# Attention and gMLP mixer on one core: five warm-up multiplications, another order in the first block, one tile moved ahead of the first heads, and one store issued earlier

## The chip, the cores and the metric

The kernel runs on 1 core of one Trainium2 chip. The metric is the device time of one execution in microseconds (us); lower is better. The time given for a kernel is the median of several runs. Beside the timed runs there is one profiled execution, from which all views are taken.

## The reference

The input is one sequence `x` of 2048 rows and 1024 columns in bf16. Two branches read it, and a gate mixes them:

```
g = sigmoid((x * gate_w).sum(-1))
a = attention(x)  @ wo        # 32 heads of 32; each row sees 8 rows: itself, 2, 4, ... 14 back
z = gelu(x @ w_in)            # 2 * 1792 columns: z1 and z2
b = (z1 * (w_sp @ layernorm(z2) + b_sp)) @ w_out     # w_sp is 2048 x 2048
out = g * a + (1 - g) * b
```

## The kernel before, in words

Everything on the chip lies in one large SBUF tile, `arena`, of which named regions are used again and again. Most of the views therefore show operands as `arena`. TensorE (PE) does the products, ScalarE (ACT) mostly the evictions from PSUM with their nonlinear function, VectorE (DVE) the attention's products and sums and the sums that the fast matrix products need; nearly all DMAs are issued by SyncE (SP), in program order.

The order of all instructions is written out by hand (`manual_schedule`): an engine runs its instructions in the order in which the Python code emits them. A small planner, `Beat`, counts the columns that PE has been given and inserts the attention's DVE steps, loads and other small work when the count reaches their due time. It knows nothing of the run; it only fixes the order.

The opening, which most of the change touches, goes as follows.

- SP issues two row tiles of x (L924), then eight pieces of the weights `w2` of z2, one for each block of 128 input rows (L926), then six row tiles of x transposed on the way (L928), the weights of the first group of heads (`load_wg(0)`, L349, three loads), the other eight row tiles of x (L931), and further loads.
- `warm_up(n)` (L115) gives PE n multiplications of a zeroed tile, 128 by 512, whose results nobody reads. They start before any data are there.
- `turn(i, h)` (L353) transposes the row tiles 0 and 1 on PE into `xT`, four blocks at a time; ACT copies one half of each tile (L359), DVE the other (L361).
- `z2_block(blocks)` (L368) computes several tiles of z2 at once: for each of the eight blocks kt of input rows, one multiplication (L374) of 128 by 448 for each tile (i, c) of the list, each into its own PSUM bank; then one eviction with gelu for each (L383). i is the row tile, c a quarter of z2's columns. `z2_tile(i, c)` is the same with one tile: eight multiplications in a row.
- Then come the tiles (2,0) to (7,0) and (2,1), with `x_abs` on DVE (L387) between them, which sums the magnitudes of two row tiles at a time.
- `qkv_tile(0, j)` (L942) is the first group of heads, one row tile j after another: eight multiplications (L947), an eviction by ACT (L950) into a staging buffer, and after every fourth tile three stores to DRAM (L955).
- After j = 13, `x_scale` (L399) spreads the sum of all magnitudes over the partitions with a one-column multiplication (L401), and DVE works out a power of two from it (L394 to L403). `x_convert(u)` (L405, L406) then turns the row tiles 2u and 2u + 1 of `xT`, in place, into scaled f16. There are eight conversions, u = 0 to 7. From then on z2 tiles read the converted rows: tile (i, c) needs conversion i // 2 and no other.
- Behind the heads come three more tiles, (3,1), (6,1) and (7,1), the transpose of the gate weights (L989), and the heads of the groups 1 and 2, whose multiplications read rows of all eight blocks at a stride. Tiles (4,1) and (5,1) follow much later (L1034).
- `bank()` (L104) hands out PSUM banks from three pools in a rotation of four, one for each tile, so the number of tiles ahead of an instruction decides which pool it takes.

The attention's DVE steps begin at a due time that is set when the first heads are emitted; they read q, k and v from DRAM (L592 to L601).

The close is the product with `w_out`, in eight groups of two row tiles (L1342 to L1384). Each group makes four quarter results `o11`, `o12`, `o21`, `o22` (row tile by column half), whose last operation on DVE is L1369 for `o22` and `finish` (L1273) for the others; a row tile is stored when both of its halves are done (L1371, L1382). In the last group the second row tile is stored in parts: the half `o22` (L1373), and two quarters of `o21` (L1377, L1378), so that little is left behind the last multiplication.

Of the kernel before, what the change touches and what calls it, by code (L numbers as in the profile page):

```python
# [15 lines left out]
P = 128  # L16
S = 2048
D = 1024
# [22 lines left out]
NU = S // 256  # L41
# [16 lines left out]
def _sub_ap(t, offset_elems, dims):  # L58
    return bass.AP(tensor=t.tensor, offset=t.offset + offset_elems, ap=[list(t.ap[0])] + [list(d) for d in dims])
# [3 lines left out]
def kernel(  # L63
# [15 lines left out]
    out2 = out.rearrange("b s d -> (b s) d")  # L79
# [24 lines left out]
    def bank():  # L104
        taken[0] += 1
        pool, tag = ((seeded, "sd"), (psum, "ps"), (second, "pd"), (psum, "ps"))[taken[0] % 4]
        return pool.tile([P, 512], F32, name=tag, tag=tag)

    def two_banks():
        return (psum.tile([P, 512], F32, name="ps", tag="ps"), second.tile([P, 512], F32, name="pd", tag="pd"))  # L110
# [4 lines left out]
    def warm_up(n):  # L115
        pw = [seeded.tile([P, 512], F32, name="pw", tag="sd") for _ in range(2)]
        for r in range(n):
            nc.tensor.matmul(pw[r % 2][:], warm[:, 0:P], warm, start=True, stop=True)
# [185 lines left out]
    sync = nc.sync  # L304
# [48 lines left out]
    def turn(i, h):  # L353
        pt = psum.tile([P, 4, P], BF, name="pt", tag="ps")
        for k in range(4):
            nc.tensor.transpose(pt[:, k, :], xn[:, i, (4 * h + k) * P:(4 * h + k + 1) * P], ident[:])
        dst = xT[:, 4 * h:4 * h + 4, i * P:(i + 1) * P]
        if h == 0:
            nc.scalar.copy(dst, pt[:])  # L359
        else:  # L360
            nc.vector.tensor_copy(dst, pt[:])  # L361

    def z2_tile(i, c, wake=False):
        z2_block([(i, c)], wake=wake)
# [3 lines left out]
    def z2_block(blocks, wake=False):  # L368
        banks = [seeded.tile([P, 512], F32, name="sd", tag="sd") if wake else bank() for _ in blocks]
        for kt in range(KT):  # L370
            for ps, (i, c) in zip(banks, blocks):
                x = xh if converted[i // 2] else xT
                N = 512 if wake and kt == 0 else ZC
                nc.tensor.matmul(ps[:, 0:N], x[:, kt, i * P:(i + 1) * P],  # L374
                                 _sub_ap(w2, kt * W2P + ZC * c, [[1, N]]),
                                 start=(kt == 0), stop=(kt == KT - 1), skip_group_check=wake)
        for ps, (i, c) in zip(banks, blocks):
            scale = xinv if converted[i // 2] else 1.0
            z2_out(ps[:, 0:ZC], i, c, scale)
            beat.run(KT * ZC)  # L380

    def z2_out(src, i, c, scale):
        nc.scalar.activation(z2[:, i, ZC * c:ZC * (c + 1)], src, ACT.Gelu_apprx_tanh, scale=scale,  # L383
                             accum_out=s1[:, 4 * i + c:4 * i + c + 1])

    def x_abs(u):
        nc.vector.tensor_reduce(xl[:, u:u + 1], tokens[u].raw, AX.XY, ALU.add, apply_absolute_value=True)  # L387
# [355 lines left out]
    def vector_steps(t):  # L743
        for item in attention_steps(t):
            if not prep["done"] and prep["normed"] == 16 and beat.vector > prep["at"]:
                for h in range(2):
                    yield 0.0, 1.25, lambda h=h: scale_rows(0, h)
                for fn in s_sums(0):
                    yield 0.0, 0.7, fn
                for fn in t_sums():  # L750
                    yield 0.0, 2.0, fn
                prep["done"] = True
            yield item
# [132 lines left out]
    def load_rows_y(u):  # L886
        for r in range(2):
            sync.dma_start_transpose(rows[u % 5].whole[r], y_d[(2 * u + r) * P:(2 * u + r + 1) * P, :])
# [69 lines left out]
        projected[g] += 1  # L958
        beat.run(KT * 3 * C)

    warm_up(6)
    for i in range(2):
        for h in range(2):
            turn(i, h)
    z2_block([(i, c) for c in range(2) for i in range(2)])
    x_abs(0)
    for i in range(2, 8):
        z2_tile(i, 0)
        if i % 2 == 1:
            x_abs(i // 2)  # L970
    z2_tile(2, 1)
    beat.steps = vector_steps(beat.now + NJ * KT * 3 * C * BEAT + 8.0)
    for j in range(NJ):
        qkv_tile(0, j)
# [8 lines left out]
                converted[u] = True  # L983
    x_convert(7)
    converted[7] = True
    for i in (3, 6, 7):
        z2_tile(i, 1)
    pt = psum.tile([P, 4, P], BF, name="pt", tag="ps")
    nc.tensor.transpose(pt[:, 0, 0:KT], gw_r[:], ident[0:KT, 0:KT])  # L989
# [122 lines left out]
    def product(ps, w, v, c0, c1, first):  # L1112
        K = v.shape[1]
        for k in range(K):
            nc.tensor.matmul(ps[:, 0:c1 - c0], w[:, k, :], v[:, k, c0:c1], start=(first and k == 0),  # L1115
                             stop=(k == K - 1), skip_group_check=True)
        beat.run(K * (c1 - c0))
# [16 lines left out]
    def fork(ps, n, bias):  # L1134
        seed = seeded.tile([P, 512], F32, name="seed", tag="sd")
        if bias is None:
            nc.scalar.copy(seed[:, 0:n], ps[:, 0:n])
        else:
            nc.scalar.activation(seed[:, 0:n], ps[:, 0:n], ACT.Identity, bias=bias)  # L1139
        return seed  # L1140
# [66 lines left out]
    for n in range(2 * NU):  # L1207
        u, fb = n // 2, n % 2
# [52 lines left out]
    def y_sums(u):  # L1261
        v = rows[u % 5]
        TT(v.s1, v.a21, v.a22, ALU.add)
        TT(v.s3, v.a11, v.a21, ALU.subtract)
        TT(v.s2, v.s1, v.a11, ALU.subtract)
        TT(v.s4, v.a12, v.s2, ALU.subtract)
# [5 lines left out]
    def finish(out, ps, scale, x):  # L1272
        nc.vector.scalar_tensor_tensor(out, ps[:], scale, x, ALU.mult, ALU.add)  # L1273

    def halves(a, views):
        return [views[2 * a + h][:, 512 * c:512 * (c + 1)] for h in range(2) for c in range(2)]
# [59 lines left out]
    def hold(ps, scale):  # L1336
        out = keeps[kept[0] % 7]
        kept[0] += 1
        nc.scalar.activation(out, ps[:], ACT.Copy, scale=scale)
        return out  # L1340

    for u in range(NU):  # L1342
        v = rows[u % 5]
        lo, hi = [omr[:, 2 * u + h:2 * u + h + 1] for h in range(2)]
        m11, m12, m21, m22 = halves(u, mix)
        o11, o12, o21, o22 = halves(u, ob_slots)
        pa, pd = two_banks()
        if u == 0:
            for n in (2, 3, 4):
                load_rows_y(n)  # L1350
        product(pa, v.a11, d11, 0, 512, True)
        pb = fork(pa, 512, None)
        product(pd, v.s1, e1, 0, 512, True)
        p5 = hold(pd, hi)
        product(pa, v.s2, e2, 0, 512, False)
        u2 = hold(pa, lo)
        product(pb, v.a12, d21, 0, 512, False)
        finish(o11, pb, lo, m11)
        TT(u2, u2, m12, ALU.add)
        product(pa, v.s3, e3, 0, 512, False)  # L1360
        u3 = hold(pa, hi)
        if u == NU - 1:
            pe = seeded.tile([P, 512], F32, name="seed", tag="sd")
            nc.scalar.copy(pe[:, 0:256], pa[:, 256:512])
        TT(p5, p5, m22, ALU.add)
        if 0 < u < NU - 1:
            y_sums(u + 1)
        product(pd, v.s4, d22, 0, 512, False)
        TT(o22, p5, u3, ALU.add)  # L1369
        finish(o12, pd, lo, u2)  # L1370
        sync.dma_start(out2[2 * u * P:(2 * u + 1) * P, :], ob_slots[2 * u])  # L1371
        if u == NU - 1:
            sync.dma_start(out2[(2 * u + 1) * P:(2 * u + 2) * P, 512:D], o22)  # L1373
            for q, ps in enumerate((pa, pe)):
                sl = slice(256 * q, 256 * (q + 1))
                product(ps, v.a22, e4, 256 * q, 256 * (q + 1), False)
                nc.vector.scalar_tensor_tensor(o21[:, sl], ps[:, 0:256], hi, m21[:, sl], ALU.mult, ALU.add)  # L1377
                sync.dma_start(out2[(2 * u + 1) * P:(2 * u + 2) * P, sl], o21[:, sl])  # L1378
        else:
            product(pa, v.a22, e4, 0, 512, False)  # L1380
            finish(o21, pa, hi, m21)
            sync.dma_start(out2[(2 * u + 1) * P:(2 * u + 2) * P, :], ob_slots[2 * u + 1])  # L1382
        if u + 5 < NU:
            load_rows_y(u + 5)  # L1384
# [30 lines left out]
```

## Time and profile before

| | |
|---|---|
| median of 3 runs | 670.32 us (670.11 to 670.51) |
| profiled execution, its own time | 671.13 us |
| its span, first to last instruction | 669.3 us |
| PE busy | 662.7 us, 99% of the span |
| DVE busy | 575.1 us, 86% |
| ACT busy | 441.9 us, 66% |

A busy PE is not PE at its peak: multiplications are pipelined, and the view gives each with its full latency, so that rows of one engine overlap. The distance between the starts of two rows is what one takes from the engine. In a timeline row the columns are start, duration, engine, line, operation, tiles, shape and count; in brackets stands the idle time of the engine just before, and what ended it. PEld is the loading of weights, SPq the issue of DMAs. In the list of waits the numbers are us in total, times, and the longest. The program's end is 1.8 us longer than the span in the profiled execution (671.13 to 669.3).

### The profile page before, as it was taken

The numbers are of one execution on the slowest core, as the hardware profiler recorded it, in microseconds if no ns is written. First come the engines' busy times: TensorE is split into PE (matmuls) and PEld (weight loads), VectorE is DVE, ScalarE is ACT, GpSimd is POOL, SyncE is SP. The second block draws the span as 40 slices with busy tenths as digits, with TensorE's granted clock in tenths as the row PEclk, the third lists the DMA queues.
The fourth block names the chain that finished last, engine by engine and source line by source line (L and its number), as shares of the span: only waits on it lengthen the run. The fifth ranks groups of instructions, "written<-read, shape, count | busy, mean of one in ns | idle before, by whom it ended". The sixth has DMA issues, their size and how long they took to land.

```text
span 669.3 us, 9594 instructions
## 1 busy us (share of the span) xinstructions
PE 662.7 (99%) x3564; PEld 389.3 (58%) x3564; DVE 575.1 (86%) x660; ACT 441.9 (66%) x774; POOL 9.4 (1%) x68
## 2 busy tenths in 40 slices
PE   8999999999999999999999999999999999999998
PEld 4558877666777777555555555555555544444443
DVE  4567999999999999999999999999978788954745
ACT  4327577888879989889755568787767774522222
POOL 0000000000001000001000000000000000000000
PEclk9999999999999999999999999999999999999999
DMA  8999593354297996994966686648589599476211
GB/s 224 182 235 255 113 227 116 105 121 120 45 283 244 279 290 203 280 327 150 292 207 213 154 217 161 166 116 229 131 211 288 142 270 225 85 167 151 54 63 64
DMA packets 229919, 123.92 MB, mean 185 GB/s; under 512 B 191088, under 2 KB 217456, under 8 KB 229872
## 3 DMA queue, kind: packets, MB, share of 16 engines
q1 hardware_dynamic: 229872, 123.31, 69.7%
q8 instruction: 28, 0.46, 0.3%
q14 instruction: 19, 0.16, 0.1%
HBM read 63.97 MB, written 37.82 MB: 152 GB/s over the span
## 4 chain that ended last, share of the span: by engine, by line
PE 97%; ACT 1%; DMA 1%; SPq 0%; issue 0%; DVE 0%
PE ps L1115 25%; PE ps L947 17%; PE pd L1115 12%; PE ps L1098 7%; PE seed L1115 7%; PE sd L947 5%; PE pd L374 4%; PE ps L455 4%; PE sd L1098 4%; PE pd L1098 4%; PE pd L947 2%; PE pd L455 2%; PE ps L374 1%; PE sd L374 1%; PE seed L455 1%; DMA arena<-in_B_w_in_dram 1%
## 5 line engine op out<-in xcount | busy, mean ns | idle before, releaser
L1115 PEld LDWEIGHTS <-arena 128*128 128x128 f16 x1519 | 148.4, 98 | 154.4 <-issue 0.7
L1115 PE MATMUL ps<-arena 128*128 128x448 f16 (+1 forms) x864 | 186.1, 363 | 0.2 <-ACT seed L1139 0.2
L947 PEld LDWEIGHTS <-arena 128*128 128x128 f16 (+1 forms) x1024 | 141.6, 139 | 30.4 <-issue 1.2
L947 PE MATMUL ps<-arena 128*128 128x384 bf16 x704 | 128.7, 326 | 0.0
L1115 PE MATMUL pd<-arena 128*128 128x448 f16 (+1 forms) x432 | 95.6, 363 | 0.0
L1098 PEld LDWEIGHTS <-arena 128*128 128x128 f16 x512 | 50.0, 98 | 46.7
L514 DVE TENSOR_TENSOR arena<-arena 128x4096 bf16<-128x4096 bf16 (+1 forms) x64 | 74.0, 1157 | 1.7
L510 DVE TENSOR_TENSOR arena<-arena 128x8192 bf16<-128x8192 bf16 x16 | 70.8, 4422 | 5.0 <-DMA arena<-k_d 4.7
L577 DVE TENSOR_TENSOR arena<-arena,att_A 128x8192 bf16<-128x8192 bf16 x16 | 70.7, 4421 | 0.2
L950 ACT CAST arena<-ps 128x384 bf16<-128x384 f32 x88 | 43.0, 489 | 23.6 <-PE ps L947 21.4
L1098 PE MATMUL ps<-arena 128*128 128x448 bf16 x256 | 53.7, 353 | 0.0
L1115 PE MATMUL seed<-arena 128*128 128x448 f16 (+2 forms) x223 | 48.7, 361 | 0.0
L947 PE MATMUL sd<-arena 128*128 128x384 bf16 x224 | 41.0, 326 | 0.8 <-ACT arena L383 0.8
L374 PEld LDWEIGHTS <-arena 128*128 128x128 f16 (+1 forms) x256 | 24.9, 98 | 23.0 <-ACT arena L359 1.1
L583 DVE TENSOR_TENSOR arena<-arena 128x4096 bf16<-128x4096 bf16 x16 | 36.6, 2287 | 0.2
L374 PE MATMUL pd<-arena 128*128 128x448 bf16 x160 | 34.7, 353 | 0.0
L1273 DVE SCALAR_TENSOR_TENSOR arena<-seed,omr,arena 128x512 bf16<-128x512 f32 x8 | 6.0, 751 | 32.7 <-PE seed L1115 32.7
L455 PEld LDWEIGHTS <-arena 128*128 128x128 f16 x224 | 21.9, 98 | 18.1 <-issue 0.5
L767 ACT ACTIVATE arena<-arena 128x2048 bf16<-128x2048 bf16 x16 | 30.9, 1932 | 0.0
L894 ACT ACTIVATE arena<-arena 128x896 bf16<-128x896 bf16 x32 | 30.3, 947 | 0.5
L455 PE MATMUL ps<-arena 128*128 128x449 f16 x128 | 29.7, 354 | 0.0
L387 DVE TENSOR_REDUCE yl<-arena 128x1 f32<-128x2048 bf16 x8 | 18.3, 2286 | 13.1 <-DMA arena<-in_A_x_dram 13.0
(207 smaller groups left out, 845.9 us busy)
## 6 DMA issues: line engine op xcount, KB each, us to landing
arena<-in_B_w_sp_dram SPq DMA_DIRECT2D x16, 512.0 KB, 4.2
arena<-v_d SPq DMA_DIRECT2D x8, 960.0 KB, 6.0
z_d<-arena SPq DMA_DIRECT2D x16, 448.0 KB, 4.5
arena<-z_d SPq DMA_DIRECT2D x16, 448.0 KB, 3.6
y_d<-arena SPq DMA_DIRECT2D x16, 448.0 KB, 4.1
arena<-k_d SPq DMA_DIRECT2D x7, 960.0 KB, 6.7
arena<-in_A_wqkv_dram SPq DMA_DIRECT2D x24, 256.0 KB, 4.6
q_d<-arena SPq DMA_DIRECT2D x32, 128.0 KB, 2.1
```

Source lines behind the costliest of these rows:

```text
L374: nc.tensor.matmul(ps[:, 0:N], x[:, kt, i * P:(i + 1) * P], _sub_ap(w2, kt * W2P + ZC * c, [[1, N]]), start=(kt == 0), stop=(kt == KT - 1) ...
L455: nc.tensor.matmul(ps[:, 0:DN - 1], lhsT, v[:, k, 0:DN - 1], start=(first and k == 0), stop=(k == 3), skip_group_check=True)
L510: TT(prod.rearrange("p (w j c) -> p w j c", w=W, j=8, c=C), in0, in1, ALU.mult)
L514: return lambda: TT(pv[:, :, 0:n], pv[:, :, 0:n], pv[:, :, n:2 * n], ALU.add)
L577: TT(prod.rearrange("p (w j d h) -> p w j d h", w=W, j=8, d=DH, h=HG), in0, in1, ALU.mult)
L583: return [(4.4, mul), (2.3, lambda: TT(p3[:, 0:4, :], p3[:, 0:4, :], p3[:, 4:8, :], ALU.add)), (1.2, lambda: TT(p3[:, 0:2, :], p3[:, 0:2, ...
L767: nc.scalar.activation(slot, slot, ACT.Abs, accum_out=l1[:, a:a + 1])
L894: nc.scalar.activation(waste, g_ring[n % 4][:, r], ACT.Abs, accum_out=yl[:, k:k + 1])
L947: nc.tensor.matmul(ps[:, 0:3 * C].rearrange("p (t c) -> p t c", t=3), lhsT, wgt[:, :, kt, :], start=(kt == 0), stop=(kt == KT - 1))
L950: nc.scalar.copy(st[:, j % 4, :].rearrange("p (t d h) -> p t d h", t=3, h=HG), ps[:, 0:3 * C].rearrange("p (t h d) -> p t d h", t=3, h=HG))
L1098: nc.tensor.matmul(ps[:, 0:512 if whole and kt == 0 else ZC], xh[:, kt, i * P:(i + 1) * P], _sub_ap(w1, kt * ZC, [[1, 512 if whole and kt ...
L1115: nc.tensor.matmul(ps[:, 0:c1 - c0], w[:, k, :], v[:, k, c0:c1], start=(first and k == 0), stop=(k == K - 1), skip_group_check=True)
```

## The change

Four edits. The warm-up has five multiplications instead of six. In the first block of z2 the four tiles are listed row tile by row tile, (0,0), (0,1), (1,0), (1,1), instead of column by column. The tile (3,1) is computed ahead of the first heads, behind (2,1), instead of behind them; it then reads the rows unconverted, and the PSUM banks of the sixteen heads are shifted by one. In the last group of the close, the half row tile `o22` is stored as soon as it is computed, ahead of the operation that finishes `o12` and of the store of the first row tile.

```diff
-    warm_up(6)
+    warm_up(5)
     for i in range(2):
         for h in range(2):
             turn(i, h)
-    z2_block([(i, c) for c in range(2) for i in range(2)])
+    z2_block([(i, c) for i in range(2) for c in range(2)])
     x_abs(0)
     for i in range(2, 8):
         z2_tile(i, 0)
         if i % 2 == 1:
             x_abs(i // 2)
-    z2_tile(2, 1)
+    for i in range(2, 4):
+        z2_tile(i, 1)
     beat.steps = vector_steps(beat.now + NJ * KT * 3 * C * BEAT + 8.0)
     for j in range(NJ):
         qkv_tile(0, j)
...
     x_convert(7)
     converted[7] = True
-    for i in (3, 6, 7):
+    for i in range(6, 8):
         z2_tile(i, 1)
...
         product(pd, v.s4, d22, 0, 512, False)
         TT(o22, p5, u3, ALU.add)
+        if u == NU - 1:
+            sync.dma_start(out2[(2 * u + 1) * P:(2 * u + 2) * P, 512:D], o22)
         finish(o12, pd, lo, u2)
         sync.dma_start(out2[2 * u * P:(2 * u + 1) * P, :], ob_slots[2 * u])
         if u == NU - 1:
-            sync.dma_start(out2[(2 * u + 1) * P:(2 * u + 2) * P, 512:D], o22)
             for q, ps in enumerate((pa, pe)):
```

Because the planner's count of PE columns stands one tile higher when the attention's due time is set, the order on DVE differs in one place: five small operations for the scale of w_in's second half (L394 to L397, L433) come ahead of one of the attention's folds (L514) instead of behind it. On ACT the eviction of (3,1) moves with its tile. Everything else keeps its order.

## The prediction

> **What bounds the kernel now.** I read the page first: busy shares, then the chain that ended last.
>
> ```profile
> PE 662.7 (99%) x3564; PEld 389.3 (58%) x3564; DVE 575.1 (86%) x660; ACT 441.9 (66%) x774; POOL 9.4 (1%) x68
> PE 97%; ACT 1%; DMA 1%; SPq 0%; issue 0%; DVE 0%
> ```
>
> PE is on the path for 97% of the span. What PE skips, or waits, is therefore the currency; other engines matter where they make PE wait. The waits of PE say where that is:
>
> ```profile
> PE pw L118 <- DVE arena L113: 1.2, 1, 1.2
> PE ps L374 <- DMA arena<-in_B_w_in_dram: 1.1, 2, 0.9
> PE sd L947 <- ACT arena L383: 0.8, 1, 0.8
> PE ps L1115 <- ACT seed L1139: 0.2, 1, 0.2
> ```
>
> There are four places only, three of them in the first 24 us. The change touches the stretch of each of these three and the last stores. So a gain has a ceiling of a few us; a loss needs a new wait.
>
> **Warm-up and order of the first block.** The timeline of the opening, the source view of the transposes, and the chain:
>
> ```profile
> 1.18 2.74 PE L118 MATMUL pw<-arena 128*128 128x512 bf16 x6 [1.18 <-DVE arena L113]
> 2.87 0.15 PEld L118 LDWEIGHTS <-arena 128*128 128x128 bf16 x1 [0.28 <-issue]
> 3.38 0.11 PEld L356 LDWEIGHTS <-arena 128*128 128x128 bf16 x1 [0.36 <-DMA arena<-in_A_x_dram]
> 3.72 1.16 PE L356 MATMUL pt<-ident,arena 128*128 128x128 bf16 x16
> L356 PE MATMUL pt<-ident,arena x16: 219/220/314, 3.7 to 4.7; 128*128 128x128 bf16 x16
> 4.24 1.07 ACT L359 COPY arena<-pt 128x512 bf16<-128x512 bf16 x2 [2.24 <-PE pt L356]
> 5.82 0.35 PE L374 MATMUL ps<-arena 128*128 128x448 bf16 x1 [0.94 <-DMA arena<-in_B_w_in_dram]
> 6.00 0.35 PE L374 MATMUL pd<-arena 128*128 128x448 bf16 x1
> 7.14 0.35 PE L374 MATMUL sd<-arena 128*128 128x448 bf16 x1
> 7.70 0.35 PE L374 MATMUL ps<-arena 128*128 128x448 bf16 x1 [0.20 <-DMA arena<-in_B_w_in_dram]
> 2.60 5.05 DMA arena<-in_B_w_in_dram
> ```
>
> A warm-up multiplication occupies PE for 0.43 us (weight loads from 1.58 to 2.87 are 0.43 apart; the last shows here). Without the sixth, PE is free at about 3.29. The transposes' weights could be loaded from 3.38, when x landed, so the transposes begin about 3.45 instead of 3.72 and their copies end about 0.25 earlier than 4.24 + 1.07 = 5.31. Nobody waits for those copies: the first multiplication starts at 5.82 on the first piece of w2, and the third piece, issued at 2.60, lands at 7.65 and restarts PE at 7.70. Neither piece waits for PE. **Removed warm-up: 0.** Its cover is the 0.94 us wait.
>
> Row tile by row tile means: in each of the eight rounds the order becomes (0,0), (0,1), (1,0), (1,1). The 32 multiplications and four results are the same; only the first two now need tile 0 alone. Tile 1 was ready by 5.31 too, half a microsecond ahead of the data. **Reordering: 0.** The bounds of both together are −0.3 (if the earlier transposes did reach PE) and +1.1 (the clock, a rival below).
>
> The clock: the trace has the first transpose at 314 ns and a median of 220, so the full clock came while the transposes started, about 3.9 us. By the 0.43 us for 512 columns, 448 columns cost 0.376 before that; from 5.82 on the spacing is 0.19. Eight multiplications fit ahead of 7.70 as long as no more than two are at the slow clock, so the grant may come as late as about 6.57. That is 2.6 us of cover.
>
> **One z2 tile moved from behind the first heads to ahead of them.** Timeline around both places, and the DMA of the heads' weights:
>
> ```profile
> 21.31 1.68 PE L374 MATMUL ps<-arena 128*128 128x448 bf16 x8
> 23.02 0.54 ACT L383 ACTIVATE arena<-ps 128x448 bf16<-128x448 f32 x1 [0.88 <-PE ps L374]
> 23.78 1.46 PE L947 MATMUL sd<-arena 128*128 128x384 bf16 x8 [0.80 <-ACT arena L383]
> 17.39 1.48 SPq L349 DMA_DIRECT2D arena<-in_A_wqkv_dram  x1
> DMA to landing us min/median/max: 6.3/6.3/6.3
> 41.98 0.17 PE L401 MATMUL ps<-rs_n,rs_b 128*128 128x1 bf16 x1
> 43.10 5.38 DVE L406 TENSOR_SCALAR arena<-arena,x_sc 128x2048 f16<-128x2048 bf16 x8
> 44.42 1.41 DVE L406 TENSOR_SCALAR arena<-arena,x_sc 128x2048 f16<-128x2048 bf16 x2
> 44.56 0.52 PEld L374 LDWEIGHTS <-arena 128*128 128x128 f16 x4 [0.18 <-DVE arena L406]
> 44.60 1.68 PE L374 MATMUL sd<-arena 128*128 128x448 bf16 x8
> 46.12 1.68 PE L374 MATMUL ps<-arena 128*128 128x448 bf16 x8
> 47.63 1.68 PE L374 MATMUL pd<-arena 128*128 128x448 bf16 x8
> 49.35 1.52 PE L947 MATMUL ps<-arena 128*128 128x384 bf16 x8
> ```
>
> Tiles follow each other by 1.51 us (46.12 to 47.63). Tile (2,1) begins at 21.31, so PE could take the next at 22.82; it waits until 23.78, a hole of 0.96. The view blames ACT, but the first head writes a bank that was read long before; what it does read are the three weight loads of L349, the last issued at 17.39 and landing 6.3 later, 23.69. So the hole is a DMA wait and a tile whose data are there fills it. Moved there, (3,1) runs 22.82 to 24.33, past the landing. **The heads start 0.55 later** (24.33 for 23.78), and all that hangs on them.
>
> Behind the heads the three tiles stood for a reason that the rows show. The scaling of x starts from the one-column multiplication L401 behind the fourteenth head; eight conversions on DVE follow from 43.10, each about 0.66 behind the last, 0.75 long. (3,1) reads block 1, converted at 44.42 + 1.41 − 2 × 0.66 = 44.51, and PEld starts at 44.56: just in time. (6,1) and (7,1) read block 3. It is the fourth conversion: it starts with the second of the x2 row, 44.42 + 0.66 = 45.08, and ends at 45.83, just before PE asked at 46.12. In the changed kernel everything from L401 is 0.55 later, so block 3 is ready at 46.38 and the weight load can start at about 46.43, the multiplication at 46.47. The heads end at 44.60 + 0.55 = 45.15. **A new wait of 1.32 us** of PE for DVE, at the first z2 tile behind the heads. What is queued behind it is all of PE's program: (7,1), the transposes of the gate weights, and every head of the second group.
>
> Sum at the second group's first head (now 49.35): +0.55 for the later start, +1.32 for the wait, −1.51 for the tile no longer there = **+0.36 us**. The conversion of the last block (43.10 + 5.38 + 0.55 = 49.03) is done before the 49.71 at which it is then asked for, so no second wait follows. The ends for the new wait are 0 (nothing is waited for) and 3.98 (a wait for all eight conversions, 49.03 + 0.10 − 45.15). I take 1.32: the 0.05 from 44.51 to 44.56 shows that the wait is on the one conversion needed.
>
> What else moves with the tile: its eviction on ACT, to a stretch where ACT waits 0.88 for every tile; the rotation of PSUM banks by one for sixteen heads; and, by the hand-kept order, five small DVE operations (the scale of w_in's second half) one fold earlier. SP's order is unchanged up to the last stores.
>
> ```profile
> 47.84 0.48 ACT L950 CAST arena<-sd 128x384 bf16<-128x384 f32 x1 [7.78 <-PE ps L374]
> 57.63 4.42 DVE L510 TENSOR_TENSOR arena<-arena 128x8192 bf16<-128x8192 bf16 x1 [4.74 <-DMA arena<-k_d]
> 75.75 1.80 ACT L437 ACTIVATE arena<-arena,yl 128x1800 f16<-128x1800 bf16 x1 [4.80 <-DVE yl L395]
> ```
>
> The thirteenth head's eviction stands until 47.84 on a staging buffer, and the transposes at about 49.5 now take its bank; it is free at 48.32, 1.2 us of cover. The attention on DVE starts at 57.63 on a DMA, 4.74 after DVE had run dry, so 0.55 on DVE costs it nothing. The fold's swap lets the conversions at 75.75 start up to 1.2 earlier, which PE doesn't wait for. These are 0. And as PE waits nowhere between there and L1115's 0.2 us, the 0.36 arrives at the end whole.
>
> **The last half row tile stored first.** The tail in narrow windows:
>
> ```profile
> 663.75 0.69 DVE L1369 TENSOR_TENSOR arena<-arena 128x512 bf16<-128x512 f32 x1 [0.28 <-ACT arena L1339]
> 664.54 0.75 DVE L1273 SCALAR_TENSOR_TENSOR arena<-pd,omr,arena 128x512 bf16<-128x512 f32 x1
> 665.36 0.33 SPq L1371 DMA_DIRECT2D out_dram<-arena  x1
> 665.78 0.38 SPq L1373 DMA_DIRECT2D out_dram<-arena  x1
> 666.07 0.48 DVE L1377 SCALAR_TENSOR_TENSOR arena<-seed,omr,arena 128x256 bf16<-128x256 f32 x1 [0.21 <-PE seed L1115]
> 666.25 0.40 SPq L1378 DMA_DIRECT2D out_dram<-arena  x1
> 666.75 0.41 SPq L1378 DMA_DIRECT2D out_dram<-arena  x1
> ```
>
> SP issues one after the other with 0.09 between (665.36 + 0.33 to 665.78; 666.25 + 0.40 to 666.75 is 0.10). The last store's data are ready at 666.55, and SP takes 0.07 from DVE's end to an issue (664.54 + 0.75 to 665.36), so it could go at 666.62: SP's queue holds it 0.13 us. In the changed kernel the half tile, ready at 664.44, is issued at about 664.51, in a stretch where SP waits; the row tile keeps 665.36, the first quarter goes at about 665.93, the last one at 666.62. **Gain 0.12.** Bounds: 0 (the bytes in flight, not the issue, set the landing) and 0.4 (one issue fewer ahead).
>
> **Sum.** 0 + 0 + 0.36 − 0.12 = +0.24 us. The profiled execution has a span of 669.3 and took 671.13 with what lies around; the median of the runs is 670.32, 0.8 below it. On the median: 670.56, a change of 0.04%. About 0.2%, 1.34 us, is what a measurement of this kernel can tell from no change.
>
> **Rivals.**
> *No new wait* (chance 0.10). If the conversions were early enough for (6,1), the filled hole stays as a gain: −0.96 − 0.12 = −1.08, 669.24. For it: the hole is real. Against it: L401 stands behind the fourteenth head in PE's order, and a tile's 1.51 between heads and (6,1) is gone.
> *Slower: the clock* (0.15). One mechanism: with PE idle about 0.1 us ahead of the transposes and 1.2 after them, the grant is not there when the first block starts. In the trace it came about 2.76 us after the first warm-up multiplication (1.18 to 3.94). Counted anew from 5.82 it comes at 8.58, after seven at 0.376 each; the eighth ends about 8.77 where PE went on at 7.70: +1.07, with the rest +1.31, 671.63. It decides from a grant later than 6.57. Against it: PE starts at the same 1.18 and works nearly without a gap to 4.6.
> The Trainium skill (TensorE: Matmul & The Clock Gate, "What's actually happening") speaks against this edit in the same place: the clock is released by activity in free-running windows of about 3.4 us, not by a count of multiplications, so less work there can miss a window. By that, as an estimate, a missed window would move the grant from 3.9 to 7.3 and cost four slow multiplications, +0.4; the trace shows one grant and no window.
> *The edits don't reach the end* (0.07): tail bound by bytes, new wait half as long, 0.2 us of slack at L1139 taken up; −0.3 to 0, 670.0 to 670.3.
> *Forecast* (0.68): 670.56, own range 670.1 to 671.0.
>
> **The numbers.** The range 669.5 to 671.7 leaves out the first rival and the far tails. Over 0.2% faster needs the first rival and 0.26 more, such as the 0.3 of a freed opening: half its chance, 0.05. Over 0.2% slower needs the clock's +1.31 with a trifle more, or a wait for all conversions: 0.12. The rest, 0.83, is within.
>
> **What would show it.** In the changed profile: PE's waits lose the 0.8 us at L947 and gain about 1.3 us at L374 behind the heads, for DVE L406; the first head at about 24.33; L401 at 42.53; (6,1) at 46.47; the second group at 49.7; first multiplication of z2 still at 5.82 and again at 7.70; the last store 0.1 us earlier relative to the last DVE operation. A first block with 0.376 spacing behind 5.82, a wait at L374 under 0.5 us, or a w2 piece landing with another time would prove the forecast wrong.

## The result, and the profile after

The changed kernel takes 671.13 us (median of 22 runs, 670.01 to 673.18), the kernel before 670.15 us (22 runs, 669.61 to 671.02). The ratio is 1.0015, 95% interval 1.0008 to 1.0022: slower by 0.15%, about 1.0 us. The forecast was +0.24 us, 670.56, with 670.1 to 671.0 as its own range and 669.5 to 671.7 as the outer one. The time lies in the outer range and above the forecast's own, the sign is the forecast one, and the size is four times the forecast. (A ratio is worked out over the runs of both kernels and is not the quotient of the two medians, so the two can differ by some hundredths of a per cent.)

The profiled execution of the changed kernel took 672.64 us with a span of 670.9, against 671.13 and 669.3 before. Its waits of PE:

```profile
PE pw L118 <- DVE arena L113: 1.2, 1, 1.2
PE ps L374 <- DVE arena L406: 1.1, 1, 1.1
PE ps L374 <- DVE arena L361: 0.6, 1, 0.6
PE ps L1116 <- ACT seed L1140: 0.2, 1, 0.2
```

The wait ahead of the first head is gone, the new one for the conversions (L406) is there, and the wait at the start of the first block is now for a copy (L361), not for w2. The timeline of PE in the opening:

```profile
1.18 2.31 PE L118 MATMUL pw<-arena 128*128 128x512 bf16 x5 [1.18 <-DVE arena L113]
3.52 1.89 PE L356 MATMUL pt<-ident,arena 128*128 128x128 bf16 x16
5.98 0.53 PE L374 MATMUL ps<-arena 128*128 128x448 bf16 x1 [0.57 <-DVE arena L361]
6.30 0.58 PE L374 MATMUL pd<-arena 128*128 128x448 bf16 x1
6.67 0.58 PE L374 MATMUL ps<-arena 128*128 128x448 bf16 x1
...
9.29 0.40 PE L374 MATMUL pd<-arena 128*128 128x448 bf16 x1
9.52 0.35 PE L374 MATMUL ps<-arena 128*128 128x448 bf16 x1
9.71 0.35 PE L374 MATMUL sd<-arena 128*128 128x448 bf16 x1
```

This is the clock, a rival of the prediction: the transposes take 1.89 us instead of 1.16, and the first block's multiplications are 0.37 apart until 9.29, then 0.19. The full clock came at about 9.4 us in this execution, where the first profile had it at 3.9. PE is 1.45 us late from here on (tile (2,1) starts at 22.76 instead of 21.31). Now the place of the moved tile and of the conversions:

```profile
22.76 1.68 PE L374 MATMUL ps<-arena 128*128 128x448 bf16 x8
24.28 1.68 PE L374 MATMUL sd<-arena 128*128 128x448 bf16 x8
25.79 0.49 PE L947 MATMUL ps<-arena 128*128 128x384 bf16 x2
...
45.31 1.46 PE L947 MATMUL sd<-arena 128*128 128x384 bf16 x8
47.90 1.69 PE L374 MATMUL ps<-arena 128*128 128x448 bf16 x8 [1.12 <-DVE arena L406]
49.42 1.68 PE L374 MATMUL pd<-arena 128*128 128x448 bf16 x8
```

The last early head starts at 45.31 and is done 1.30 later, at 46.61; (6,1) starts at 47.90. The wait is 1.29 us; 1.32 was forecast. (The view counts 1.12, from the latency end of the row before.) At the tail, the issues of SP and the last operation of DVE:

```profile
666.25 0.33 SPq L1372 DMA_DIRECT2D out_dram<-arena  x1
667.10 0.33 SPq L1374 DMA_DIRECT2D out_dram<-arena  x1
667.85 0.48 DVE L1379 SCALAR_TENSOR_TENSOR arena<-seed,omr,arena 128x256 bf16<-128x256 f32 x1 [0.21 <-PE seed L1116]
668.36 0.33 SPq L1380 DMA_DIRECT2D out_dram<-arena  x1
```

From the start of the last DVE operation to the last issue it is 0.51 us (667.85 to 668.36), where it was 0.68 (666.07 to 666.75), and to the end of the span 3.02 instead of 3.27 (the spans are 670.86 and 669.34 with two decimals). So this one execution adds up: +1.45 in the opening, +0.34 at the second group's first head (51.14 there, 49.35 before, less the 1.45), −0.25 at the tail. That is +1.54 for a span that grew by 1.52. But 672.64 is the third longest of the 22 runs, and the sum of one execution is not the sum of the median. That is what the experiments had to separate.

### The profile page after: what moved, and what is told of

Its sections match the earlier page's. It is cut to its first block, busy times and chain, and to the rows that moved or that the text cites. A ratio compares the mean times of both kernels' runs of the same rounds, so it can differ in the third digit from the quotient of the medians.

```text
span 670.9 us, 9591 instructions
## 1 busy us (share of the span) xinstructions
PE 664.7 (99%) x3563; PEld 390.1 (58%) x3563; DVE 574.9 (86%) x660; ACT 443.1 (66%) x774; POOL 9.4 (1%) x68
## 4 chain that ended last, share of the span: by engine, by line
PE 98%; ACT 1%; DVE 1%; issue 0%
PE ps L1116 25%; PE ps L947 17%; PE pd L1116 12%; PE ps L1099 7%; PE seed L1116 7%; PE sd L947 5%; PE pd L374 5%; PE ps L455 4%; PE sd L1099 4%; PE pd L1099 4%; PE pd L947 2%; PE pd L455 2%; PE ps L374 2%; PE sd L374 1%; PE seed L455 1%; DVE arena L406 0%
## 5 line engine op out<-in xcount | busy, mean ns | idle before, releaser
L514 DVE TENSOR_TENSOR arena<-arena 128x4096 bf16<-128x4096 bf16 (+1 forms) x64 | 74.0, 1157 | 1.7
L1128 ACT ACTIVATE arena<-ps,bt 128x448 f32<-128x448 f32 x32 | 20.2, 632 | 13.9 <-PE ps L1116 13.4
```

The source lines that it names most:

```text
L514: return lambda: TT(pv[:, :, 0:n], pv[:, :, 0:n], pv[:, :, n:2 * n], ALU.add)
```

## The experiments

First each edit by itself. **Only the warm-up**, on the kernel before:

```diff
-    warm_up(6)
+    warm_up(5)
```

> The kernel before with five warm-up multiplications and nothing else changed. Theory A (the clock): with one multiplication less the full clock comes a whole window later in part of the executions, the transposes and the first block then run at 0.107 and 0.376 us a piece for some us. It expects about +0.7 us on the median (0.3 to 1.2), a spread of the runs over 2 us where the kernel before had 1.4, and a fastest run no slower than the fastest before. Theory B (the moved tile carries all of it): 0, within 0.2.

Measured: 669.85 us to 670.05 before, ratio 1.0000, interval 0.9991 to 1.0009; 669.47 to 670.76 in eleven runs. The clock as the cause of the median, theory A, is out. Its own profile shows why the missing multiplication need not cost anything:

```profile
5.64 0.53 PE L374 MATMUL ps<-arena 128*128 128x448 bf16 x1 [0.28 <-ACT arena L359]
5.97 0.58 PE L374 MATMUL pd<-arena 128*128 128x448 bf16 x1
6.34 0.58 PE L374 MATMUL ps<-arena 128*128 128x448 bf16 x1
6.71 0.53 PE L374 MATMUL sd<-arena 128*128 128x448 bf16 x1
7.08 0.35 PE L374 MATMUL ps<-arena 128*128 128x448 bf16 x1
...
21.45 1.68 PE L374 MATMUL ps<-arena 128*128 128x448 bf16 x8
22.97 1.46 PE L947 MATMUL sd<-arena 128*128 128x384 bf16 x8
```

The clock came at about 7 us and cost next to nothing, since the block still ended about where it did. And the last two rows show something that the forecast had not reckoned with: tile (2,1) starts at 21.45, the first head at 22.97, 1.52 later. There is no hole ahead of the heads here.

**All but the warm-up**: the changed kernel with `warm_up(6)`.

> The changed kernel with the six warm-up multiplications put back. Theory A: what is left is the wait behind the heads and the tail, +0.35 - 0.2 = +0.1 to +0.3 us, with the spread of the kernel before. Theory B: nearly all of the change's +1.0 us stays.

Measured: 671.14 us, ratio to before 1.0014 (1.0005 to 1.0023). The whole loss is there with all six warm-up multiplications; its profile has the clock by 6.7 us and the same 1.1 us wait for L406.

**Only the tile**, on the kernel before:

```diff
-    z2_tile(2, 1)
+    for i in range(2, 4):
+        z2_tile(i, 1)
...
-    for i in (3, 6, 7):
+    for i in range(6, 8):
```

> The kernel before with tile (3,1) moved ahead of the first heads and nothing else changed. Theory A: +0.36 us: a wait of 1.3 us for the fourth conversion behind the heads, against 0.96 us of hole filled. Theory B: +1.0 or more. A third possibility, that the wait in the profile is paid for by time that PE loses elsewhere anyway, expects -0.9 to 0.

Measured: 671.05 us, +1.0, ratio 1.0017 (1.0008 to 1.0025). The moved tile carries the loss: the "+1.0 or more" of theory B, not the +0.36 of the forecast. Tenths of a us are beyond these medians of eleven runs: this kernel, without the earlier store, should lie above "all but the warm-up" by what the store is worth, and lies 0.09 below it.

**Only the order of the block and the store**:

> The kernel before with the other order in the first block and the half row tile stored first, nothing else changed. Theory A and B alike: the order 0, the store -0.1 to -0.2 us. If the order by row tiles matters for the opening, the first multiplication of the first block starts earlier than 5.8 us or the block ends earlier than 12.2 us.

Measured: 669.88 us, −0.17, ratio 1.0000 (0.9991 to 1.0009). By the medians alone the difference is not clear of the noise; the tail shows it in all fourteen profiles: from the start of the last DVE operation to the end of the span it is 3.27 or 3.28 us in the five profiles with the old order of stores, and 3.01 to 3.03 in the nine with the new one. The store is worth 0.25 us. In this run's profile the first block starts at 6.09 and waits for w2, which is issued as before.

Then theory C was formed: the hole of 0.96 us that the tile was to fill is not there in most executions, and so the wait of 1.3 us is paid in full. **The kernel before once more**, for its profile:

> The kernel before once more, for its profile alone. Theory C: the heads' weights are there when PE gets to them, no hole ahead of the first head (the first profile had 0.96 us). Theory D: the hole is there again.

The issue of the last of the three weight loads, what the view of that tensor says of landing, and PE's rows:

```profile
16.83 1.60 SPq L349 DMA_DIRECT2D arena<-in_A_wqkv_dram  x1
```

```profile
DMA to landing us min/median/max: 5.3/5.3/5.3
```

```profile
21.02 1.68 PE L374 MATMUL ps<-arena 128*128 128x448 bf16 x8
22.53 1.46 PE L947 MATMUL sd<-arena 128*128 128x384 bf16 x8
```

No hole: the last weights are issued at 16.83 and land 5.3 later, at 22.13, ahead of the 22.53 at which PE asks. In the first profile it was 23.69 against 22.82. Worked out in the same way for all fourteen profiles, the weights land ahead of the end of tile (2,1) in twelve, in those of the kernels with the moved tile too; they are late in the first profile and in one further below (e12). This execution took 669.87 us, 1.26 less than the first profiled one, and the hole of 0.96 is most of that.

**The wait taken away**, on the changed kernel, by working the scale out two heads earlier, which the sum of x permits:

```diff
-        if j == 13:
+        if j == 11:
             x_scale()
-            for u in range(7):
+            for u in range(6):
                 x_convert(u)
                 converted[u] = True
+        if j == 13:
+            x_convert(6)
+            converted[6] = True
```

> The changed kernel with the scale of x worked out behind the twelfth head instead of the fourteenth: conversions 0 to 5 start about 2.6 us earlier, conversion 6 follows the fourteenth head and 7 the sixteenth as before. Theory C (the moved tile costs because its 1.51 us of cover behind the heads turn into a wait for the fourth conversion, while the hole that it was to fill is an accident of single executions): no wait at L374 behind the heads, the second group starts about 1.3 us earlier than in the changed kernel relative to the first heads, and the time falls by 1.1 to 1.3 us below the changed kernel, to about the kernel before or 0.2 below it. Theory D (the wait only shows where time is lost anyway; the cost is the shift of all later work against DVE and the DMAs): the wait goes, the time stays at +1.0.

Measured: 669.66 us to 670.12 before, ratio 0.9998 (0.9989 to 1.0006). The loss of 1.0 us is gone, and 0.46 of the medians' difference lies on the other side, though the interval spans no change. Its PE waits hold no L406 any more, and the tile follows the heads at once:

```profile
42.55 5.38 DVE L406 TENSOR_SCALAR arena<-arena,x_sc 128x2048 f16<-128x2048 bf16 x8
```

```profile
45.35 1.46 PE L947 MATMUL sd<-arena 128*128 128x384 bf16 x8
46.65 1.68 PE L374 MATMUL ps<-arena 128*128 128x448 bf16 x8
48.16 1.68 PE L374 MATMUL pd<-arena 128*128 128x448 bf16 x8
```

From the first head to the second group's first head it is 24.05 us here and 25.35 in the changed kernel: the 1.3 of the wait. So the cost was the wait itself; theory D falls.

**Only the order of the conversions**, block 3 first, on the changed kernel:

```diff
-            for u in range(7):
+            for u in (3, 0, 1, 2, 4, 5, 6):
```

> The changed kernel with the conversion of block 3 first, ahead of 0, 1, 2, 4, 5, 6. Theory C: (6,1) starts at once, but the second group needs all eight conversions, which end 5.4 us after the first starts; a wait of 0.8 to 0.9 us appears at its first head, and only about 0.5 us is won of the changed kernel's loss: +0.5 us to before. If the order alone were the fault, all of it, 1.3 us, would come back.

Measured: 670.41 us to 670.12, ratio 1.0007 (0.9998 to 1.0016). By the medians some 0.7 of the loss comes back and 0.3 stays, though the interval reaches no change; in the profile 0.6 comes back (24.76 us from the first head to the second group's, for 25.35). The wait turns up where it was expected, smaller than reckoned:

```profile
PE ps L947 <- DVE arena L406: 0.6, 1, 0.6
```

The second group needs all eight conversions: 1.1 us from L401 to the first (41.98 to 43.10 in the first profile) and 5.4 from there, 6.5 in all. Two heads of 1.30 us and two tiles of 1.51 give 5.6 of cover, three tiles 7.1. That is what the third tile was worth behind the heads.

**One warm-up multiplication**, on the kernel before, to size the clock:

> The kernel before with one warm-up multiplication instead of six. It measures the clock term: if the grant of the full clock follows PE's work by windows, one multiplication leaves PE idle until 3.4 us, the grant comes more often behind 7 us, and the median rises by 0.5 to 1.5 us with a spread over 2 us. If the grant doesn't depend on the warm-up, 0.

Measured: 671.15 us, +1.0, ratio 1.0018 (1.0010 to 1.0026), 669.83 to 673.02. In its profile the spacing of the first block falls from 0.37 to 0.19 only at about 8.5 us. So the warm-up does its work. Over all runs with five multiplications (four kernels) 6 of 55 lay 1.4 us or more above the median of their set; with six (six sets of variants and five of the kernel before) it was 3 of 194. Of the six, the two that have a profile, the changed kernel's first and e7's, show the clock at 9.4 us. For the other four, and for the three with six multiplications, the cause is inferred, not shown.

Last, a version without the wait and with the full warm-up, in three forms on one chip. **Early scale, tile ahead, six warm-ups**:

> The changed kernel with the early scale of x and six warm-up multiplications again. Theory C with the clock as a matter of single executions: the median as with five, 0.25 to 0.5 us below the kernel before (the tail is worth 0.25), and no run over 1 us above its own median, where 6 of 55 runs with five warm-ups lay 1.4 us or more above. If five warm-ups cost every execution something, the median falls further, by 0.3 us or more.

Measured: 669.92 us to 670.72 before, ratio 0.9987 (0.9978 to 0.9996), 669.14 to 670.42. It is faster than the kernel before on the same chip, and no run is 1 us over its median; the changed kernel, at a ratio of 1.0015, was measured apart from it. **The same with the tile behind the heads**:

> The kernel before with the early scale of x, the other order in the first block and the half row tile stored first; six warm-ups, tile (3,1) behind the heads. Theory C: without the wait for the conversions the place of the tile is worth nothing in executions without a hole, so within 0.2 us of the kernel with the tile ahead. If the hole ahead of the heads is common, the kernel with the tile ahead is faster by 0.4 us or more.

Measured: 670.52 us, ratio 0.9997 (0.9988 to 1.0006), 0.6 slower than with the tile ahead. That is what was expected if the hole is common on this chip, where the kernel before takes 670.72 and not 670.1, and this kernel's profile has it:

```profile
20.86 1.68 PE L374 MATMUL ps<-arena 128*128 128x448 bf16 x8
23.01 1.46 PE L947 MATMUL sd<-arena 128*128 128x384 bf16 x8 [0.48 <-DMA arena<-in_A_wqkv_dram]
```

From 20.86 to 23.01 it is 2.15 us for a tile of 1.51: a hole of 0.64, and here the view names the weights' DMA as what ended it. So theory C needs a correction: the hole isn't an accident of one execution. It comes and goes with two times, that of the landing and that at which PE asks. Here the weights land at about 22.9, no later than in the changed kernel's profile, but PE asks at 22.37 (20.86 + 1.51), the earliest of all profiles. That holes make the whole difference of 0.6 is not shown: in the other three profiles known to be from this chip the weights land in time, and this profile and that of the version with the tile ahead reach the second group at the same time (48.58 and 48.60). **Eight warm-ups**:

> The same as the first of this set with eight warm-up multiplications. They end 0.86 us later than six, so the transposes and their copies end at 6.0 to 6.8 us, behind the landing of w2's first piece: +0.3 to +0.8 us on the median, with no late grant of the clock. If the copies still end ahead of the data, 0.

Measured: 670.23 us, ratio 0.9993 (0.9984 to 1.0002), 0.3 above the one with six, with the smallest spread of all, 669.83 to 670.42. **The best version again**:

> The kernel with early scale, the tile ahead and six warm-ups once more, on whatever chip comes. If its gain is the tail plus the hole that the kernel before has in some executions, it lies 0.25 us below the kernel before where that one runs without a hole (a median near 670.1) and 0.5 to 0.9 below where holes are common (a median near 670.7); its own spread stays under 1.5 us.

Measured: 670.01 us to 670.43, ratio 0.9992 (0.9984 to 1.0001), 669.63 to 670.84. Of the two measurements of this version one is clear of no change and one just not; both lie between the two ends of what was expected.

## Why the prediction was right or wrong

- *Removed warm-up: 0.* Right for the median (e1). The rival beside it was real: in single executions the clock comes late. It was priced at +1.07 and cost 1.45 in the profile, because the slow transposes also put off the first multiplication (5.98, now on a copy) and nine multiplications ran slow, not seven. "PE starts at the same 1.18 and works nearly without a gap" was no protection: the grant came anywhere from 3.9 to 9.4 us. And the wait for w2 that was to be the cover stands ahead of the first multiplication in only five of the fourteen profiles. By the prediction's own signs the 0.37 spacing in the changed profile speaks against the forecast; it belongs to that execution, and what moved the median was another step.
- The rule of the Trainium skill (TensorE: Matmul & The Clock Gate, "What's actually happening"), free-running windows of activity, agrees in kind: the same program got its clock at different times, the kernel before at 3.9 us in one profile and, by the spacing of the first rows, near 5.9 in the other. The one missed window of the estimate, 7.3 us, is near the 7.1 of e1's profile; the two late executions that have a profile show 9.4.
- *Reordering: 0.* Right.
- *Hole filled, −0.96.* Wrong, and this is the step that failed. It was read off one profiled execution. That execution had taken 671.13 us, 0.8 above the median of the timed runs, and the prediction wrote the difference down and added its sum to the median all the same. An execution longer than the median by just about the hole was the hint that the hole wasn't in the median; 671.13 is above the longest of the 22 timed runs, 671.02. Read against that one profile the sum was good: +0.36 forecast and +0.34 found at the second group's first head. Without the hole the heads start 1.51 us later, not 0.55, and the sum at the second group is 1.29 in place of 0.36.
- *New wait, 1.32.* Right in place, cause and size: 1.29 in three profiles.
- *Tail, −0.12.* Right in mechanism, half the size: 0.25. Besides the 0.17 that the last issue comes earlier, that issue itself takes 0.33 where it took 0.41.
- With the hole at 0 and the tail at 0.25 the same working gives 1.29 − 0.25 = +1.04; +0.98 was measured. That it fits to 0.06 is in part luck: the moved tile alone should by this have cost 1.29, and 1.0 was measured. Where those 0.3 went is open; holes in some runs of the kernel before would explain them, and no run shows how many had one. It is luck too that the time lies in the outer range, whose upper end leaves room for the clock's +1.31 (671.63); none of the prediction's rivals has the hole missing.
- *The banks, ACT, SP and the attention: 0.* Right: apart from the opening, the conversions and the tail, no wait of PE changed. From the second group's first head to the end of the span it is 619.97 to 620.00 us in the five profiles with the old order of stores and 619.72 to 619.75 in the nine with the new one. Whatever else differs between these fourteen executions lies in the first 52 us.

## What to carry to other kernels

Ask of every idle stretch in a profile whether the median has it: compare the profiled execution's own time with the timed runs before putting a hole into a sum, above all a hole that a DMA ends. Work that stands between a producer and its consumer is cover, even where the view shows no wait there: before moving it, add up the whole chain that it hides. And a chain that can start earlier is better than cover: two heads' earlier start of the scale made the moved tile free.

## What the runs showed of the hardware

The time at which TensorE's full clock is granted differs by over 5 us between executions of nearly the same opening. By the traces' granted clock it lay between 3.9 and 6.8 us in the seven profiles with six warm-up multiplications that record it, at 4.3, 7.1, 9.4 and 9.4 in the four with five, and at 8.6 in the one with one. These ranges overlap, so a single profile doesn't tell what one multiplication is worth; over the runs it was 3 of 194 with six and 6 of 55 with five that lay 1.4 us or more above their median, and a median 1.0 us higher with one. The landing of one and the same load of weights took 5.3 us in one execution of the kernel before and 6.3 in another. That is enough to open or close a hole of 0.96 us; whether the chips differ in it is not shown.
